# Sums of the value weights on POOL, other places for splits, statistics and x sums, and the feature minimum taken from the differences

## The chip, the core and the metric

The kernel runs on one core of a Trainium2 chip. The core has five engines with queues of their own: TensorE (PE; its weight loads are shown as PEld), VectorE (DVE), ScalarE (ACT), GpSimd (POOL) and SyncE (SP), which here only issues transfers; ACT issues a few too. Each engine works off its instructions in order and waits on semaphores for the others. The metric is device time in microseconds (us) of the whole kernel.

## The reference: what is computed

For 2048 tokens of width 640, the reference normalizes x and lets two branches work on it. The first is linear attention with 32 heads of 20: queries and keys go through a small matrix per head and a double softmax, and the sums over all tokens of (key feature times value) and of the key features give the output. The second is a two-layer GELU network of width 1536. The result is x + s * silu(g).

```
xn = _layernorm(x, axis=-1)
phi_q = concatenate([_softmax(pq), _softmax(-pq)]);  phi_k likewise     # per head, over 20
kv = einsum("bhsf,bhsd->bhfd", phi_k, v);  z = einsum("bhsf->bhf", phi_k)
o  = (phi_q kv) / (phi_q z + 1e-6);        s = o @ wo
g  = silu(gelu(xn @ w1 + b1) @ w2 + b2)
return x + s * g
```

## The kernel before

Everything is float32 in value, but TensorE works on pairs of fp32r halves: a tile is copied rounded by ACT (high half), and DVE or POOL subtract to get the rest (low half); `PASSES` multiplies high by high, high by low and low by high. "Split" below means this pair of instructions.

The tokens are worked off in 16 tiles of 128; a pair q is tiles 2q and 2q+1. Tiles 0 to 9 are projected one by one (`project`, 30 matmuls of 320 columns). For tiles 6 to 9 each turn t does a key tile, a value tile and two query tiles. From tile 10 on (passes p = 5, 6, 7, the loop over `range(5, 8)`), keys are still done tile by tile, but the values of a pair are done together in `token_pair` by a scheme of seven products (parts X, Y, X, V, Z, W, Z) on sums and differences of weights and of x. The same scheme then does the queries of pairs 4 to 7, and the feed-forward part over 12 units fills the rest of the time.

For the scheme, four sums of the value weights are made by `v_forms(0)` and `v_forms(1)` (each loads two 128-row blocks, makes four sums of 320 columns and stores the blocks to `sv_dram`). `forms` reloads them as four tiles and splits them, one per `next`: the first two are the tiles `ws` of parts Y and V, the last two go partly into the old `wv` tiles (part W) and partly into a third `ws` (the second part Z). The query weights take the same way through `sq_dram`; `w_dump` stores two `wq` tiles for a later reload. For x, `pair_stats` makes a tile's mean and variance (DVE) and reciprocal deviation (POOL, a power), sends both through `st_dram` and reads them back on all partitions as `bc`; `pair_sub` (POOL) and `pair_mul` (DVE) normalize the pair `xr`; `pair_plain` splits it into `xp`; `t_sums` (five POOL instructions) makes its x sums and `t_split` splits them into `xd`.

`feat1` makes the exponents of a tile from the PSUM tile `pA`: per head maximum `mx` and minimum `mn`, differences to the maximum, `nr` = minimum less maximum, and on POOL the second half (`nr` less differences); `feat2` is ACT's exponential, `key_fin` the division by the sums (the product on POOL). There are three PSUM tiles `pA` in turn (`bankA`); TensorE can start a fourth projection only when the features, or ACT's eviction of a value tile, have read the oldest.

Order: TensorE's and SP's instructions in this phase go out as the program writes them (`manual_schedule` on these two engines). On DVE, ACT and POOL, Tile's scheduler sets the order from the program and its own estimate; from the feed-forward part on, all is as written. In `value_pair(p, {...})` the dictionary hooks pieces of other work behind numbered parts of the scheme.

## Time and profile before

Times are device microseconds.

| | |
|---|---|
| median of 3 runs | 663.66 (662.34 to 664.63) |
| profiled execution | 663.49, of which 661.4 is the span from the first to the last instruction |
| mean granted TensorE clock | 0.994 of full |
| busy in the span: PE, PEld | 648.8 (98%), 562.4 |
| DVE, ACT, POOL | 501.6 (76%), 237.4 (36%), 395.5 (60%) |
| moved by DMA | 135.15 MB, 204 GB/s mean |

How to read what follows: a row of the timeline gives start, duration, engine, line of the program, operation, output and inputs, shapes and how many instructions are merged; in brackets, how long the engine had been idle before and whose work ended that. The duration of merged rows is from the first start to the last end; a single instruction's duration overlaps the next one's by some 0.08 us. "SPq" and "ACTq" rows are transfers being issued. In the chain of waits, each piece is what released the next. A line "a/b/c" gives the shortest, median and longest duration in ns.

### The profile page before, as it was taken

The numbers are of one execution on the slowest core, as the hardware profiler recorded it, in microseconds if no ns is written. First come the engines' busy times: TensorE is split into PE (matmuls) and PEld (weight loads), VectorE is DVE, ScalarE is ACT, GpSimd is POOL, SyncE is SP. The second block draws the span as 40 slices with busy tenths as digits, with TensorE's granted clock in tenths as the row PEclk, the third lists the DMA queues.
The fourth block names the chain that finished last, engine by engine and source line by source line (L and its number), as shares of the span: only waits on it lengthen the run. The fifth ranks groups of instructions, "written<-read, shape, count | busy, mean of one in ns | idle before, by whom it ended". The sixth has DMA issues, their size and how long they took to land.

```text
span 661.4 us, 11452 instructions
## 1 busy us (share of the span) xinstructions
PE 648.8 (98%) x4396; PEld 562.4 (85%) x4396; DVE 501.6 (76%) x777; ACT 237.4 (36%) x345; POOL 395.5 (60%) x351
## 2 busy tenths in 40 slices
PE   9999999989799999999999999999999999999997
PEld 9999999989799998888888888888888887766866
DVE  5785977998887988758978868859789899853232
ACT  3512322413534256352442444841322425132130
POOL 2755475787586855857778776363462967343321
PEclk9999999999799999999999999999999999999999
DMA  9706297533811168628799699796779399999952
GB/s 349 273 1 175 83 345 227 128 123 124 198 58 42 70 227 290 210 76 282 194 278 324 154 402 323 128 327 241 147 214 244 85 266 183 310 232 254 299 208 79
DMA packets 164447, 135.15 MB, mean 204 GB/s; under 512 B 89394, under 2 KB 128562, under 8 KB 164010
## 3 DMA queue, kind: packets, MB, share of 16 engines
q1 hardware_dynamic: 161658, 122.84, 63.6%
q10 hardware_dynamic: 2736, 11.60, 5.3%
q8 instruction: 34, 0.56, 0.4%
q14 instruction: 19, 0.16, 0.1%
HBM read 86.03 MB, written 48.38 MB: 203 GB/s over the span
## 4 chain that ended last, share of the span: by engine, by line
PE 81%; DVE 5%; DMA 5%; POOL 4%; issue 2%; SPq 1%; ACT 1%; ACTq 0%; DVEq 0%; POOLq 0%
PE pB L909 24%; PE pB L880 22%; PE pA L371 11%; PE pB L1067 11%; PE pA L653 5%; DMA st_dram<-pst 2%; PE pB L1014 2%; PE pA L174 1%; POOL xr L301 1%; PE qV L653 1%; PE kv L453 1%; DMA folds<-in_wqk_dram 1%; POOL e L414 1%; POOL e L392 1%; PE qY L653 1%
## 5 line engine op out<-in xcount | busy, mean ns | idle before, releaser
L909 PE MATMUL pB<-hs,w2s 128*128 128x512 f32 x720 | 165.8, 389 | 0.0
L909 PEld LDWEIGHTS pB<-hs,w2s 128*128 128x128 f32 x720 | 135.0, 188 | 28.8 <-DVE y L918 0.8
L880 PE MATMUL pB<-xp,w1s 128*128 128x512 f32 x324 | 81.4, 390 | 0.0
L880 PE MATMUL pB<-xd,w1s 128*128 128x512 f32 x324 | 79.3, 389 | 0.0
L1067 PE MATMUL pB<-oT,wo 128*128 128x512 f32 (+1 forms) x315 | 72.3, 381 | 0.0
L880 PEld LDWEIGHTS pB<-xp,w1s 128*128 128x128 f32 x324 | 60.7, 188 | 12.8 <-DVE pB L1148 0.3
L880 PEld LDWEIGHTS pB<-xd,w1s 128*128 128x128 f32 x324 | 60.8, 188 | 12.6
L414 POOL TENSOR_TENSOR eq<-eq,rc 128x1280 f32<-128x1280 f32 x16 | 37.9, 2370 | 55.9 <-DVE rc L971 38.7
L1067 PEld LDWEIGHTS pB<-oT,wo 128*128 128x128 f32 x315 | 57.2, 188 | 13.8 <-PE pB L1014 2.5
L918 DVE TENSOR_TENSOR y<-pB,y 128x512 f32<-128x512 f32 x100 | 63.1, 675 | 1.4 <-PE pB L909 1.4
L401 ACT ACTIVATE e<-e 128x1280 f32<-128x1280 f32 x32 | 40.6, 1270 | 65.5 <-POOL e L392 65.5
L392 POOL TENSOR_TENSOR e<-nr,e 128x640 f32<-128x640 f32 x32 | 46.4, 1449 | 23.5 <-DVE nr L391 18.0
L414 POOL TENSOR_TENSOR e<-e,rc 128x1280 f32<-128x1280 f32 x16 | 39.2, 2450 | 35.0 <-DVE rc L441 35.0
L371 PE MATMUL pA<-wk,xp 128*128 128x320 f32 x384 | 59.7, 310 | 0.3 <-ACT v L430 0.3
L885 ACT ACTIVATE pB<-pB,b1t 128x512 f32<-128x512 f32 x48 | 31.8, 662 | 78.7 <-DVE pB L1148 28.9
L371 PEld LDWEIGHTS pA<-wk,xp 128*128 128x128 f32 x384 | 56.9, 188 | 0.7 <-ACT v L430 0.6
L958 POOL TENSOR_TENSOR ez<-eq,zrep 128x1280 f32<-128x1280 f32 x16 | 47.3, 2959 | 1.4 <-DMA eq<-e_dram 1.4
L481 POOL TENSOR_TENSOR w1s<-raw,w1s 128x640 fp32r<-128x640 f32 (+1 forms) x18 | 26.8, 1489 | 31.9 <-ACT w1s L480 31.9
L371 PE MATMUL pA<-wv,xp 128*128 128x320 f32 x240 | 37.7, 311 | 0.0
L371 PEld LDWEIGHTS pA<-wv,xp 128*128 128x128 f32 x240 | 35.5, 188 | 0.1
L1070 POOL TENSOR_TENSOR xres<-gt,xres 128x256 f32<-128x256 f32 x20 | 14.3, 737 | 35.3 <-DVE gt L1069 24.8
L891 DVE TENSOR_TENSOR hs<-pB,hs 128x512 fp32r<-128x512 f32 x48 | 32.0, 683 | 3.9 <-ACT hs L887 3.7
(182 smaller groups left out, 1159.8 us busy)
## 6 DMA issues: line engine op xcount, KB each, us to landing
raw<-in_w_dram SPq DMA_DIRECT2D x42, 320.0 KB
e_dram<-e ACTq DMA_DIRECT2D x16, 640.0 KB
eq<-e_dram SPq DMA_DIRECT2D x16, 640.0 KB
phi_t<-eq SPq DMA_DIRECT2D x64, 160.0 KB
phT<-phi_t SPq DMA_DIRECT2D x20, 480.0 KB
xt<-in_x_dram SPq DMA_DIRECT2D x16, 320.0 KB
xres<-in_xt_dram SPq DMA_DIRECT2D x20, 256.0 KB
out_dram<-xres SPq DMA_DIRECT2D x18, 256.0 KB
```

Source lines behind the costliest of these rows:

```text
L371: nc.tensor.matmul(ps[:, hf, :HALF], stat_x(q, o, k, a), ws[k][:, b, hf * HALF:(hf + 1) * HALF], start=n == 0, stop=n == 3 * KC - 1)
L392: rest = lambda: nc.gpsimd.tensor_tensor(e5[:, :, :, 1, :], nr[:, :, :, None].to_broadcast([P, 2, 16, DH]), e5[:, :, :, 0, :], op=OP.subtract)
L401: nc.scalar.activation(ef, ef, AF.Exp)
L414: nc.gpsimd.tensor_tensor(e3, e3, rc[:, :, None].to_broadcast([P, 64, DH]), op=OP.mult)
L653: nc.tensor.matmul(bank[ch], q_x(blk, a, q), p_weight(base, f, w, k)[:, b], start=ch not in seen and n == 0, stop=n == len(mms) - 1, skip_ ...
L880: nc.tensor.matmul(bank[ch][:], tl[:, a, off + wo_:off + wo_ + P], mov(blk, b), start=new and n == 0, stop=n == len(mms) - 1, skip_group_c ...
L885: nc.scalar.activation(ps, ps, AF.Gelu_apprx_tanh, bias=b1t[:, f:f + 1])
L891: nc.vector.tensor_tensor(hs[:, 1], ps, hs[:, 0].bitcast(F32), op=OP.subtract)
L909: nc.tensor.matmul(ps[:], ws[i][:, b, d * P:(d + 1) * P], hs[o][i][:, a, :], start=i == n == 0, stop=(i, n) == (GF - 1, 2), skip_group_che ...
L918: nc.vector.tensor_tensor(y, ps[:], y, op=OP.add)
L958: nc.gpsimd.tensor_tensor(zv, ef, zf, op=OP.mult)
L1067: nc.tensor.matmul(ps[:, mv], w, o[:, mv], start=n == 0, stop=n == 15, skip_group_check=True)
```

## The change

1. `v_forms`: both groups of four sums run on POOL (before, the second ran on DVE). The second group's loads and sums go to turn 6 (before: turns 7 and 8).
2. `feat1`: the minimum over `pA` and the subtraction of two 128x32 tiles go; instead `nr` is the minimum over the differences `e`, read from SBUF. The result is the same, since subtracting the maximum keeps the order.
3. `XIN`, `STATS`: tiles 14 and 15 are loaded at the end of turn 7 (before 8), their statistics made in turn 8 (before 9).
4. Turns 7 to 9: `t_sums` comes behind the first query's features. In turn 9, the first two splits of the reloaded sums are made there (before in pass p=5), ahead of `t_split`; in pass p=5 one fewer in the hook and one fewer behind the key.
5. `w_dump`: both stores of `wq` go to turn 9, behind the reload of the sums (before: turns 6 and 7).
6. Pass p=7: the last of the four query splits is POOL's and comes at part 2 (before DVE, part 5).

```diff
 def v_forms(i):
-        eng = nc.vector if i else nc.gpsimd
-        put = lambda d, x, y, op: eng.tensor_tensor(d, x, y, op=op)
+        put = lambda d, x, y, op: nc.gpsimd.tensor_tensor(d, x, y, op=op)
...
 def feat1(ps, later=None):
-        mn = small.tile([P, 2, 16], F32, tag="mn", name="mn")
         nc.vector.tensor_reduce(mx[:], p4, axis=AX.X, op=OP.max)
-        nc.vector.tensor_reduce(mn[:], p4, axis=AX.X, op=OP.min)
...
-        last_feat[0] = nc.vector.tensor_tensor(nr[:], mn[:], mx[:], op=OP.subtract)
+        last_feat[0] = nc.vector.tensor_reduce(nr[:], e5[:, :, :, 0, :], axis=AX.X, op=OP.min)
...
-    XIN = {6: (12, 13), 8: (14, 15)}
-    STATS = {6: (10, 11), 7: (12, 13), 9: (14, 15)}
+    XIN = {6: (12, 13), 7: (14, 15)}
+    STATS = {6: (10, 11), 7: (12, 13), 8: (14, 15)}
...
         if t == 9:
             vb = forms(sv_dram, wv_f, wv_s, [nc.vector] * 4)
             next(vb)
+            w_dump(0)
+            w_dump(1)
         if t == 6:
+            next(vf[1])
             spill(3)
...
+        pq = project(next(queries), wq_s)
+        ef = feat1(pq)
         if t > 6:
             t_sums(q - 1)
-        pq = project(next(queries), wq_s)
-        ef = feat1(pq)
         if t < 9:
             pair_mul(q)
-        if t in (7, 8):
-            next(vf[1])
...
         ef = feat1(pq)
+        if t == 6:
+            next(vf[1])
+        if t == 9:
+            next(vb)
+            next(vb)
         if t > 6:
             t_split(q - 1)
...
-        if t in (6, 7):
-            w_dump(t - 6)
...
-            qf = forms(sq_dram, wq_f, wq_b, [nc.vector] * 4)
+            qf = forms(sq_dram, wq_f, wq_b, [nc.vector, nc.vector, nc.vector, nc.gpsimd])
...
         if p == 5:
             load_xr(7)
             next(vb)
-            next(vb)
...
         def rest(t=t, p=p):
-            if p == 5:
-                next(vb)
...
-        value_pair(p, {0: lambda: p == 5 and next(vb), 1: rest, 5: lambda: p == 7 and next(qf), 4: first_key, 6: second_key})
+        value_pair(p, {0: lambda: p == 5 and next(vb), 1: rest, 2: lambda: p == 7 and next(qf), 4: first_key, 6: second_key})
```

TensorE's instructions keep their order. On the others, three places matter. In the rows below, `mx`, `mn`, `e` and `nr` belong to one feature computation, `xr<-xr,bc` is the multiplication of a pair, `raw<-raw` the sums of the value weights, `st` and `pst` the statistics.

DVE in turn 8, before: between the first and the second query's features.

```order
L345 TENSOR_TENSOR xr<-xr,bc 128x1280
L214 TENSOR_TENSOR raw<-raw 128x320 x4
L384 TENSOR_REDUCE mx<-pA 128x32
L385 TENSOR_REDUCE mn<-pA 128x32
L388 TENSOR_TENSOR e<-pA,mx 128x32x20
L391 TENSOR_TENSOR nr<-mn,mx 128x32
```

The same place after the change (the last four rows stand there once more, for the second tile, and then come the second query's features):

```order
L344 TENSOR_TENSOR xr<-xr,bc 128x1280
L230 BN_STATS st<-xt 128x6 x2
L231 BN_AGGR st<-st 128x2
L232 TENSOR_SCALAR pst<-st 128x1
L235 COPY pst<-st 128x1
```

The sums have left DVE, the statistics of tiles 14 and 15 (from turn 9) stand there.

ACT from the first query of turn 9 into pass p=5, before (`e` is an exponential, `xd` the x split, `ws` and `wv` the copies of the reloaded sums, `qx` the copy of a PSUM part):

```order
L401 ACTIVATE e<-e 128x1280
L685 DMA e_dram<-e 128x1280
L322 ACTIVATE xd<-xr 128x9x128
L401 ACTIVATE e<-e 128x1280
L685 DMA e_dram<-e 128x1280
L609 ACTIVATE ws<-raw 128x640 x2
L657 ACTIVATE qx<-pA 128x320
L609 ACTIVATE wv<-raw 128x320
L609 ACTIVATE ws<-raw 128x320
```

The same place after:

```order
L398 ACTIVATE e<-e 128x1280
L682 DMA e_dram<-e 128x1280
L606 ACTIVATE ws<-raw 128x640 x2
L321 ACTIVATE xd<-xr 128x9x128
L398 ACTIVATE e<-e 128x1280
L682 DMA e_dram<-e 128x1280
L606 ACTIVATE wv<-raw 128x320
L606 ACTIVATE ws<-raw 128x320
L654 ACTIVATE qx<-pA 128x320
```

The copies of the first two sums have moved ahead of the x split and of the second exponential, and those of the third ahead of the copy of the first PSUM part.

POOL in turn 8, before (`xr<-xr` are the x sums, `e<-nr,e` the second half of the exponents, `e<-e,rc` the key product):

```order
L414 TENSOR_TENSOR e<-e,rc 128x1280
L301 TENSOR_TENSOR xr<-xr 128x2x128 x4
L301 TENSOR_TENSOR xr<-xr 128x128
L392 TENSOR_TENSOR e<-nr,e 128x32x20 x2
L323 TENSOR_TENSOR xd<-xr,xd 128x9x128
L392 TENSOR_TENSOR e<-nr,e 128x32x20
```

The same place after:

```order
L411 TENSOR_TENSOR e<-e,rc 128x1280
L389 TENSOR_TENSOR e<-nr,e 128x32x20
L300 TENSOR_TENSOR xr<-xr 128x2x128 x4
L300 TENSOR_TENSOR xr<-xr 128x128
L233 TENSOR_TENSOR pst<-pst,mhalf 128x1 x2
L389 TENSOR_TENSOR e<-nr,e 128x32x20
L322 TENSOR_TENSOR xd<-xr,xd 128x9x128
L389 TENSOR_TENSOR e<-nr,e 128x32x20
```

The first query's exponents come ahead of the x sums, and the two powers of the statistics come between the sums and the second query's exponents.

## The prediction

> **What bounds the kernel now.** I read the page first, then busy time by stretches, then what TensorE waited for, then the rows around those waits.
>
> ```profile
> span 661.4 us, 11452 instructions
> PE 648.8 (98%) x4396; PEld 562.4 (85%) x4396; DVE 501.6 (76%) x777; ACT 237.4 (36%) x345; POOL 395.5 (60%) x351
> ```
>
> TensorE is busy for 648.8 of 661.4 us, so only its 12.6 us of idle time and any slowed clock can be won. The next view cuts the span into stretches; the columns are the length, then the busy time of PE, weight loads, DVE, ACT and POOL, and the granted clock.
>
> ```profile
> core 0: us, PE busy (x) PEld busy (x) DVE busy (x) ACT busy (x) POOL busy (x), PEclk, DMA share, GB/s
> 165.00:176.40 11.40, 7.68 (x32) 6.67 (x33) 8.50 (x12) 8.38 (x13) 7.64 (x9) 0.70 0.96 212
> 300.00:661.40 361.40, 357.07 (x1588) 283.54 (x1586) 263.67 (x402) 124.07 (x186) 204.54 (x156) 1.00 0.83 235
> ```
>
> The last 361 us lose 4.3 us, at the end, and the change does not reach there. The sore place is 165 to 176.4: TensorE sits idle for 3.7 us and then runs at clock 0.70. Next, all waits of TensorE's matmuls in its middle part (total, times, longest):
>
> ```profile
> PE qY L653 <- ACT ws L609: 2.6, 1, 2.6
> PE pA L371 <- DVE nr L391: 2.0, 1, 2.0
> PE qY L653 <- DVE ws L610: 1.1, 2, 0.6
> PE pA L653 <- DVE pA L667: 1.0, 1, 1.0
> PE pA L371 <- ACT v L430: 0.3, 1, 0.3
> ```
>
> So three places count: 143 us (a bank that the features free late), 165 us (split weights `ws`), 223 us (a sum in the first query pair). TensorE's order of instructions is the same in both kernels; what the change can do is take away such waits or make new ones.
>
> **Place B, the splits of the sums of the value weights.** TensorE, the chain of waits, ACT and DVE:
>
> ```profile
> 154.57 4.67 PE L371 MATMUL pA<-wk,xp 128*128 128x320 f32 x30 [0.34 <-ACT v L430]
> 179.91 8.80 PE pA L371 x60
> 198.15 8.80 PE pA L371 x60
> 163.40 1.28 ACT L401 ACTIVATE e<-e 128x1280 f32<-128x1280 f32 x1 [8.88 <-POOL e L392]
> 167.88 1.36 ACT L609 ACTIVATE ws<-raw 128x640 fp32r<-128x640 f32 x2 [0.48 <-ACT e L401]
> 168.65 2.85 DVE L610 TENSOR_TENSOR ws<-raw,ws 128x640 fp32r<-128x640 f32 x2 [2.90 <-ACT ws L609]
> ```
>
> Pass p=5 (two key tiles, one sum into kv, one value pair) runs on TensorE from 154.57 to 179.91, 25.34 us; pass p=6, the same matmuls, from 179.91 to 198.15, 18.24 us. The 7.1 us between them are what late `ws` costs, slow clock included. ACT stood idle 8.88 us for POOL and only then worked off exponentials, x splits and `ws` in order. After the change statistics 14 and 15 are gone from DVE there, POOL makes the second operand of the first query's exponential ahead of the x sums instead of behind them, ACT copies `ws` ahead of the x split and of the second query's exponential, and DVE splits `ws` ahead of key tile 10's features. If `ws` is then in time: -7.1.
>
> **Place A, sums of the value weights off DVE.**
>
> ```profile
> 137.35 5.51 DVE L214 TENSOR_TENSOR raw<-raw 128x320 f32<-128x320 f32 x4
> 158.52 0.87 DVE L231 BATCH_NORM_STATS2 st<-xt 128x6 f32<-128x320 f32 x2
> 161.08 0.81 DVE L384 TENSOR_REDUCE mx<-pA 128x32 f32<-128x640 f32 x1
> 145.20 4.63 PE L371 MATMUL pA<-wq,xp 128*128 128x320 f32 x30 [2.00 <-DVE nr L391]
> ```
>
> The four sums fill 137.35 to 142.86; only then come the features whose bank TensorE needs at 143.2. In their place now stand statistics 14 and 15, 2.56 us (158.52 to 161.08), so those features start near 139.9 and release the bank (behind maximum and difference) about 1.6 us later, 141.5. The 2.0 us wait goes: -2.0.
>
> On POOL the four sums go in at tile 6, behind the second query's exponent operand. POOL's time for the first pair's sums is in the trace, and its cover is its idle time before the x subtraction of the next pair:
>
> ```profile
> L214 POOL TENSOR_TENSOR raw<-raw x4: 878/882/888, 77.5 to 80.4; 128x320 f32<-128x320 f32 x4
> 110.25 2.99 POOL L340 TENSOR_TENSOR xr<-xr,bc 128x1280 f32<-128x1280 f32 x1 [3.86 <-issue]
> ```
>
> Four of them cost between 3.5 us (0.88 each) and 5.5 us (the DVE row above, taken in turns with POOL); I take 3.5, POOL's own row. They fill that gap, cost 0. Without the gap they would move the x subtraction and all behind it on POOL by as much. The loads are issued on SP ahead of two stores of `xp`; the two stores of `wq` leave the place between the broadcasts `bc` and go behind the reload of the sums. Nobody reads them before p=7, so both cost 0.
>
> What speaks against it is that DVE instructions with two SBUF inputs can stand still while POOL works (rows below), so that sums on POOL may cost DVE what they save it. By the rows the gain stays: what is freed is DVE's queue ahead of a bank that TensorE needs, while POOL's turn for the sums lies some 30 us earlier, where TensorE waits for nothing. The Trainium skill, "Perfetto Trace Analysis", section "Optimizing Scalar/DVE Operations", says that moving work between DVE and GPSIMD might not help because they share an SBUF port; by that rule A would give 0 and the sum below would be 2.0 us worse.
>
> **The minimum from the differences.** A reduction from PSUM and a tiny subtraction, 32 times each, become one reduction of the differences in SBUF, which stands third instead of second.
>
> ```profile
> L391 DVE TENSOR_TENSOR nr<-mn,mx x32: 174/180/2670, 21.3 to 255.1; 128x32 f32<-128x32 f32 x32
> L409 DVE TENSOR_REDUCE rc<-e x16: 1472/1480/1487, 29.2 to 220.9; 128x64 f32<-128x1280 f32 x16
> 124.64 2.70 POOL L323 TENSOR_TENSOR xd<-xr,xd 128x1152 fp32r<-128x1152 f32 x1 [0.62 <-ACT xd L322]
> 124.71 2.67 DVE L391 TENSOR_TENSOR nr<-mn,mx 128x32 f32<-128x32 f32 x1
> ```
>
> The subtraction takes 0.18 us but up to 2.67, exactly as long as the POOL instruction that had started before it. A reduction that reads one SBUF tile (L409, 1280 numbers) takes 1.472 to 1.487 us in all 16 cases, under POOL or not. So the new reduction of 640 numbers lies between 0.74 us (half of L409) and 1.48 (strided reads at half speed); I take 0.81, what the maximum of the same count takes from PSUM (row 161.08), nearest in size. Feature time without POOL stays about 2.3 us, and the stretched cases shrink by up to 2.5 us. The bank is free one instruction (0.73 us) earlier. None of this is on TensorE's path by itself, so it counts 0 in the sum, and it is the margin for what follows.
>
> **Place C, the last quarter of the query splits on POOL.**
>
> ```profile
> 216.85 2.60 DVE L610 TENSOR_TENSOR wqb<-raw,wqb 128x320 fp32r<-128x320 f32 x1
> 219.37 1.17 DVE L610 TENSOR_TENSOR ws<-raw,ws 128x320 fp32r<-128x320 f32 x1
> 223.92 1.14 PE L653 MATMUL pA<-ws,xp 128*128 128x320 f32 x6 [0.96 <-DVE pA L667]
> 216.74 2.37 POOL L414 TENSOR_TENSOR e<-e,rc 128x1280 f32<-128x1280 f32 x1 [3.87 <-DVE rc L441]
> ```
>
> DVE loses 3.6 us of work right ahead of the sum that TensorE waits 0.96 us for; POOL takes two instructions in a gap of 3.87 us. -1.0. Without the gap the key product behind them is late, which TensorE reads only two query pairs on.
>
> **What is late next.** POOL is now the tight queue of tiles 8 and 9. Its rows, and ACT's eviction of the last value tile:
>
> ```profile
> 132.92 2.99 POOL L340 TENSOR_TENSOR xr<-xr,bc 128x1280 f32<-128x1280 f32 x1 [3.67 <-DMA wq_dram<-wq]
> 135.99 3.67 POOL L414 TENSOR_TENSOR e<-e,rc 128x1280 f32<-128x1280 f32 x1
> 148.11 2.69 POOL L323 TENSOR_TENSOR xd<-xr,xd 128x1152 fp32r<-128x1152 f32 x1 [1.60 <-ACT xd L322]
> 158.50 3.63 POOL L301 TENSOR_TENSOR xr<-xr 128x256 f32<-128x256 f32 x5
> 162.09 1.28 POOL L392 TENSOR_TENSOR e<-nr,e 128x640 f32<-128x640 f32 x1
> 163.32 1.06 POOL L234 TENSOR_TENSOR pst<-pst,mhalf 128x1 f32<-128x1 f32 x2
> 153.83 0.68 ACT L430 ACTIVATE v<-pA 128x640 f32<-128x640 f32 x1
> ```
>
> Laid end to end in the new order from 135.9: key product 3.67, operand 1.28, x sums 3.63, powers 1.06, operand 1.28, x split 2.69, operand of key 9 1.28: 150.8. ACT's exponential (1.28) and the eviction follow: 152.8. TensorE wants that bank for key tile 10 at 154.57 - 0.34 - 2.0 = 152.2. A wait of 0.6 stands where 0.34 stood: +0.3. From 152.1 DVE makes key 9's sums (1.48 and a reciprocal, to 154.1), POOL the product, the operand, the x sums and the next operand (about 8.6 us, to 162.7), ACT an exponential, two half copies and the copy of bank X, to 165.4. TensorE, at key 10 from 152.8, wants bank X again at 152.8 + 8.8 (both key tiles) + 1.5 (the kv sums, what pass p=6 has left beside 60 and 54 matmuls at 8.80 / 60 each) + 1.8 (parts X and Y) = 164.9: +0.5. `ws` itself is there earlier: ACT copies it behind the first query's exponential near 160.5, DVE is through by 163, and part Y starts near 163.9. These 0.8 us vanish if `bc` lands sooner without the store of `wq` behind it, which is the wait that row 132.92 names, and double if POOL meets DVE more often.
>
> The reloaded sums must also be there. They now stand behind the last statistics on SP:
>
> ```profile
> 88.91 5.09 DMA xt<-in_x_dram
> 164.41 0.37 SPq L332 DMA_DIRECT2D st_dram<-pst  x1
> 169.61 0.32 SPq L334 DMA_DIRECT2D bc<-st_dram  x1
> ```
>
> Powers end near 145.5, the store's round trip to `bc` takes 5.2 us, four issues about 2, a load 5.1: 157.8, against ACT's turn near 159.
>
> **The sum.** -2.0 (A) - 7.1 (B) - 1.0 (C) + 0.3 + 0.5 = -9.3. The profiled execution took 663.49 us (2.1 around its span; 0.17 under the median 663.66): 654.2.
>
> **Rivals.** *The stall moves to POOL's chain.* For it: POOL is in order and each operand now waits for more. Against: every wait above is under 1 us. If half of place B comes back, 3.5 us: 657.7. From 2 to 6 us lost: 656 to 660.5. *The reduction is dear* (1.48 us). Then each feature costs 0.7 more on DVE, ten of them between 133 and 165 cost 7, and 661 to 662 results; L409's even rows speak against it. *POOL holds DVE up:* the sums at tile 6 cost DVE's x splits 3.5 us in waits as in row 124.71, and the bank at 143 is as late as before: 656.2. *Slower:* the reloads of the sums land late, behind `bc` on SP's in-order queue. Part Y wants `ws` near 163.9, and copy and split need some 4 us after the landing; each us past 160 is lost on TensorE, and a wait of 3.7 us drew 7.1 - 3.7 = 3.4 us of slow clock with it in the row of 165 to 176.4. A landing at 166 (6 us of wait and 3.4 of slow clock) eats the whole gain; at 169 the time is 666.5. The loads would have to take 13 us in place of 5.1.
>
> **How the numbers follow.** Forecast 0.72 (652.6 to 656), moved stall 0.14, dear reduction 0.04 (no change), POOL holding DVE up 0.04 (655 to 657), slower 0.06. The low end is all waits gone and no new one (653.4) less the spread of runs; the high end, 658.5, takes in half of B. Faster by over 0.3% (2 us, about what runs of this kernel tell apart): 0.90; within it 0.04; slower 0.06.
>
> **What would show it.** Right: TensorE's waits on `ws` gone, passes p=5 and p=6 equally long, clock 1.00 throughout, the new reduction at about 0.8 us in all 32 cases with no long ones, the wait at 143 gone. Wrong: TensorE waiting on ACT's copy of bank X or on `ws` behind a DMA, POOL without idle time from 133 to 165, or a reduction well over 0.8.

## The result

The changed kernel takes 660.65 us (median of 13 runs, 659.70 to 662.23), the kernel before 664.45 (13 runs beside them): ratio 0.9954, 95% interval 0.9941 to 0.9967: a gain of 3.8 us by the medians and of 3.1 us by the ratio. Forecast were 654.2 us and a range up to 658.5. The direction was right, the size was not, and the time lies outside the range.

The profiled execution of the changed kernel took 661.99 us. From its page, the span and the busy times; then TensorE's waits in its middle part (total, times, longest):

```profile
span 660.3 us, 11417 instructions
PE 649.2 (98%) x4396; PEld 562.6 (85%) x4396; DVE 493.0 (75%) x739; ACT 237.6 (36%) x345; POOL 399.2 (60%) x357
```

```profile
PE pA L370 <- DVE e L385: 2.3, 2, 1.9
PE pA L650 <- ACT qx L654: 1.5, 2, 1.0
PE pA L650 <- DVE wv L607: 1.0, 1, 1.0
PE pA L650 <- DVE v L664: 0.9, 2, 0.6
```

The waits for `ws` and the wait at 223 us are gone, as forecast. The wait near 143 us is still there (1.86 us at 146.17), pass p=5 has new ones for `qx`, `wv` and `v`, and pass p=6 has two. TensorE's timeline shows where:

```profile
146.17 6.17 PE L370 MATMUL pA<-wq,xp 128*128 128x320 f32 x30 [1.86 <-DVE e L385]
156.57 4.56 PE L370 MATMUL pA<-wk,xp 128*128 128x320 f32 x30
169.34 1.58 PE L650 MATMUL pA<-wv,xp 128*128 128x320 f32 x9 [0.52 <-ACT qx L654]
173.84 1.89 PE L650 MATMUL pA<-wv,xd 128*128 128x320 f32 x11 [1.02 <-DVE wv L607]
176.31 1.15 PE L650 MATMUL pA<-ws,xp 128*128 128x320 f32 x6 [0.58 <-DVE v L664]
177.74 4.56 PE L370 MATMUL pA<-wk,xp 128*128 128x320 f32 x30
190.94 1.58 PE L650 MATMUL pA<-wv,xp 128*128 128x320 f32 x9 [0.95 <-ACT qx L654]
```

Pass p=5 runs from 156.57 to 177.74, 21.17 us (before: 25.18 by the same rows). Pass p=6 runs from 177.74 to 197.75, 20.01 us (before: 18.24, without a wait). The span is only 1.1 us shorter than before; two more profiles of the changed kernel, taken with the experiments, have spans of 660.8 and 658.6. The next table puts three of the four side by side. Its first row is the start of POOL's product for key tile 9, for a reason that the experiments give; the spans between are worked out from the starts of the rows named.

| us | before | changed, first profile | changed, third profile |
|---|---|---|---|
| POOL's product of key 9 starts | 156.18 | 156.84 | 155.16 |
| from there to the end of pass p=5 | 23.57 | 20.90 | 20.89 |
| pass p=6 | 18.24 | 20.01 | 20.01 |
| pass p=7 and the queries, to the feed-forward part | 52.62 | 51.43 | 51.42 |
| feed-forward part and end | 410.79 | 411.12 | 411.12 |
| span | 661.4 | 660.3 | 658.6 |

The change won 2.7 us behind POOL's product (place B) and 1.2 us in the queries (place C), lost 1.8 in pass p=6, and moved the product itself by +0.7 or -1.0 (place A was to bring it 2 us forward). The profiled execution of before (663.49 us) and the third of the changed kernel (660.32) lie 3.2 us apart, the first one (661.99) only 1.5; the medians, 3.8. The profiled execution of before is 0.96 us under its kernel's median of 13, and the first of the changed kernel 1.34 us above its own, which makes up the difference. Not all of the gain lies in the instructions, either: outside the span, the kernel before spends 2.1 us on average and the changed kernel 1.7. No run shows why.

### The profile page after: what moved, and what is told of

The parts are those of the page before. It is cut to its first block, busy times and chain, and to the rows that moved or that the text cites. A ratio compares the mean times of both kernels' runs of the same rounds, so it can differ in the third digit from the quotient of the medians.

```text
span 660.3 us, 11417 instructions
## 1 busy us (share of the span) xinstructions
PE 649.2 (98%) x4396; PEld 562.6 (85%) x4396; DVE 493.0 (75%) x739; ACT 237.6 (36%) x345; POOL 399.2 (60%) x357
## 4 chain that ended last, share of the span: by engine, by line
PE 84%; DVE 6%; POOL 5%; ACT 1%; issue 1%; DMA 1%; SPq 0%; ACTq 0%; DVEq 0%; POOLq 0%
PE pB L907 24%; PE pB L878 21%; PE pA L370 14%; PE pB L1065 11%; PE pA L650 5%; PE pA L174 2%; PE pB L1012 2%; POOL e L389 2%; POOL e L411 1%; POOL xr L300 1%; DVE xp L287 1%; PE qV L650 1%; PE kv L450 1%; ACT e L398 1%; DVE rc L406 1%
## 5 line engine op out<-in xcount | busy, mean ns | idle before, releaser
L478 POOL TENSOR_TENSOR w1s<-raw,w1s 128x640 fp32r<-128x640 f32 (+1 forms) x18 | 25.0, 1391 | 29.4 <-ACT w1s L477 23.3
```

## The experiments

Each kernel was run in five rounds beside the kernel before on the same chip, except the third profile of the changed kernel, which is a single execution. "Ratio" is to the kernel before; "product" is the start of POOL's product of key 9, "behind it" the time from there to the end of pass p=5. Each ratio comes from 6 to 12 executions of the kernel, while span, product and passes are those of one profile. Every kernel in the table, whatever its edit, spends 1.7 to 1.8 us outside its span and the kernel before 2.1, so that 0.3 to 0.4 us (about 0.0005 of the ratio) speak for each of them without any change between the first instruction and the last. Where it matters, the mean span of all executions is given beside the ratio.

| kernel | ratio (95%) | span | product | behind it | p=6 |
|---|---|---|---|---|---|
| changed, again | 0.9956 (0.9939 to 0.9973) | 660.8 | 157.37 | 20.88 | 20.01 |
| x sums of turn 7 early | 0.9976 (0.9965 to 0.9987) | 659.3 | 155.87 | 20.95 | 19.96 |
| x sums of turns 7 to 9 early | 1.0013 (1.0002 to 1.0024) | 661.6 | 156.22 | 22.84 | 19.96 |
| sums on POOL alone | 1.0008 (0.9995 to 1.0021) | 662.8 | 157.74 | 23.01 | 18.24 |
| split on DVE | 0.9988 (0.9975 to 1.0000) | 663.3 | 159.77 | 20.98 | 20.01 |
| x sums of turn 9 late | 0.9947 (0.9932 to 0.9962) | 659.4 | 156.74 | 20.05 | 19.95 |
| all three | 0.9927 (0.9912 to 0.9942) | 656.4 | 156.24 | 19.56 | 18.35 |
| eviction first | 0.9929 (0.9907 to 0.9950) | 656.5 | 156.21 | 19.54 | 18.40 |
| `wv` splits first | 0.9918 (0.9900 to 0.9936) | 656.2 | 155.82 | 19.16 | 18.80 |
| query split alone | 0.9981 (0.9968 to 0.9994) | 661.1 | 156.40 | 24.17 | 18.23 |
| old minimum | 0.9950 (0.9934 to 0.9966) | 658.0 | 156.31 | 20.99 | 18.35 |
| minimum alone | 1.0020 (1.0009 to 1.0030) | 662.2 | 155.14 | 23.34 | 19.71 |
| operand held | 0.9988 (0.9976 to 1.0000) | 661.0 | 157.54 | 20.92 | 19.97 |
| operand held, second form | 0.9924 (0.9907 to 0.9940) | 658.2 | 156.29 | 20.92 | 18.44 |

### The wait near 143 us: a buffer, and then POOL

DVE's timeline of the changed kernel, turn 8. The second query of turn 7 has its maximum at 118.88, but its differences start only here:

```profile
124.79 0.82 DVE L385 TENSOR_TENSOR e<-pA,mx 128x640 f32<-128x640 f32 x1 [5.09 <-DMA e_dram<-e]
132.55 3.46 DVE L287 TENSOR_TENSOR xp<-xr,xp 128x384 fp32r<-128x384 f32 x1
144.35 0.81 DVE L382 TENSOR_REDUCE mx<-pA 128x32 f32<-128x640 f32 x1
```

They waited 5.09 us for a store: their tile `e` (from the pool of 23 large buffers) got the buffer of the first query's `e`, which is free only when that one is stored. In the kernel before the differences of that query start at 121.69 without such a wait. Which buffer a tile gets is decided by Tile when it sets the order, and moving `t_sums` behind the first query's features is enough to change it, as the next run shows. First theory: this wait is why the gain of place A is missing. The test moves the x sums of turn 7 back:

```
-        pq = project(next(queries), wq_s)
-        ef = feat1(pq)
-        if t > 6:
+        if t == 7:
+            t_sums(q - 1)
+        pq = project(next(queries), wq_s)
+        ef = feat1(pq)
+        if t > 7:
             t_sums(q - 1)
```

> The changed kernel, with the x sums of turn 7 alone back ahead of the first query's features; turns 8 and 9 as changed. Theory S (buffer): in the changed kernel the differences `e` of turn 7's second query get the buffer of the first query's `e` and wait 5.09 us on DVE for that tile's store; the wait at 139.2 (0.48 us), the one at 144.3 (1.86 us) and the 1.5 us of slow clock behind it are its price. In this order the differences take another buffer: the 5.09 us are gone although the first query's store is issued later, TensorE's waits between 139 and 147 fall under 0.5 us in all, and pass p=5 starts near 153 instead of 156.6: 656.7 (4 us less than 660.65). Rival L (lock): DVE is late there because POOL's instructions with two SBUF inputs hold its splits (3.46 us for one of 0.55); then the wait at 144 stays above 1 us and the time within 1 us of 660.65.

The mechanism came out as expected, the time did not. TensorE and ACT of that kernel:

```profile
154.26 4.66 PE L370 MATMUL pA<-wk,xp 128*128 128x320 f32 x30 [2.07 <-ACT v L427]
168.37 1.58 PE L650 MATMUL pA<-wv,xp 128*128 128x320 f32 x9 [1.76 <-ACT qx L654]
```

```profile
152.35 1.27 ACT L398 ACTIVATE e<-e 128x1280 f32<-128x1280 f32 x1 [1.30 <-POOL e L389]
153.52 0.69 ACT L427 ACTIVATE v<-pA 128x640 f32<-128x640 f32 x1
```

Between 100 and 154 us TensorE now has no wait at all. It waits 2.07 us at 154 instead, for ACT's eviction of v9, which stands behind an exponential that waited for POOL; and `qx` costs 1.76 in place of 0.52. The ratio, 0.9976, is no better than the changed kernel's. Rival L fares no better: DVE's last split took 0.55 us here. With the x sums early in turns 8 and 9 too (`if t > 6` in place of `if t == 7` above, and the second call gone) the result is worse still:

> The changed kernel with the x sums of turns 7, 8 and 9 back ahead of the first query's features. Theory S: the 5.09 us wait on DVE is gone as in the run with turn 7 alone (-4), but in turn 9 POOL makes the operand of the first query's exponential some 3.6 us later, ACT's copies of `ws` come that much later, and part Y waits up to 3 us for them: 657 to 660. If the order in turn 9 is of no use to place B, 656.7 as with turn 7 alone. Rival L: 660 to 664.

It took 663.42 us, 1.0013 of the kernel before. The late x sums of turns 8 and 9 are therefore worth 1.9 us behind POOL's product (22.84 against 20.95, slow clock included), and behind that product only those of turn 9 stand: that part of the forecast for place B holds.

Second theory, P: not TensorE but POOL's in-order queue, with ACT and DVE in between, sets the pace from 112 to 175 us; TensorE has slack there, and a wait of it is worth nothing. One test is place A alone: the kernel before, with only the second group of sums on POOL in turn 6.

```
 def v_forms(i):
-        eng = nc.vector if i else nc.gpsimd
-        put = lambda d, x, y, op: eng.tensor_tensor(d, x, y, op=op)
+        put = lambda d, x, y, op: nc.gpsimd.tensor_tensor(d, x, y, op=op)
...
         if t == 6:
+            next(vf[1])
             spill(3)
...
-        if t in (7, 8):
-            next(vf[1])
...
         ef = feat1(pq)
+        if t == 6:
+            next(vf[1])
```

> The kernel before, with only the second group of sums of the value weights on POOL in turn 6 (place A alone; the queries' and statistics' order, the minimum and all splits as before). Prediction's count for A: the wait of 2.00 us at 145.2 goes and nothing comes back, -2.0. Theory P (POOL's chain is the bound right behind it): the wait at 145 goes, but TensorE, earlier by as much, waits longer for v9's eviction (0.34 before) and for `ws` (3.7 before): less than 1 us is won. Rival from the Trainium skill, Perfetto Trace Analysis, section Optimizing Scalar/DVE Operations (a move between DVE and GPSIMD might not help): by that rule 0 too, but then with the wait at 145 still in place.

The wait of 2.00 us at 145 is gone, and a larger one stands at the next place (TensorE's timeline):

```profile
156.13 6.91 PE L370 MATMUL pA<-wk,xp 128*128 128x320 f32 x30 [4.43 <-ACT v L429]
```

Ratio 1.0008 (mean span 0.7 us longer than before): place A alone won nothing. The forecast's cited rule (the Trainium skill, "Perfetto Trace Analysis", section "Optimizing Scalar/DVE Operations") gave 0 too, and the measurement agrees with that result; but the wait at 145 did go.

Two things took the gain back, and this run does not separate them. One is theory P: the eviction that TensorE waits for stands behind POOL's operand. The other is a cost that the forecast set to 0, the loads of the second group, which SP now issues earlier. Pair 5's statistics are ready at 98.74 us before and at 98.45 here, but SP is still at work on what stands ahead of their store (SP's queue, before and place A alone):

```profile
98.77 0.37 SPq L332 DMA_DIRECT2D st_dram<-pst  x1
```

```profile
100.44 0.91 SPq L331 DMA_DIRECT2D st_dram<-pst  x1
```

POOL's x subtraction, which needs them back, starts at 112.75 in place of 110.25, and the product of key 8 at 138.19 in place of 135.99; the chain of waits of this kernel runs over these transfers. All 14 profiles with the moved loads, those of the changed kernel included, issue this store 0.2 to 2.4 us after the statistics are ready, the three without them (before, query split alone, minimum alone) 0.02 to 0.03 us after. What place A would be worth without this delay, no run shows. DVE's splits beside the moved sums had a smaller price: in turn 7 of the changed kernel they took 0.95, 1.10 and 1.63 us (0.82, 0.42 and 0.56 before).

The chain of waits shows theory P without an experiment. Of the changed kernel, in order of time:

```profile
138.14 2.30 POOL e L411
...
151.43 1.86 POOL e L389
153.31 1.28 ACT e L398
154.62 1.50 DVE rc L406
...
156.84 2.37 POOL e L411
...
173.31 0.49 DVE wv L607
173.84 1.91 PE pA L650 x11
```

From 112.9 to 173.8 it holds no piece of TensorE. The same view of the kernel before was there to be read:

```profile
136.04 3.62 POOL e L414
...
150.80 1.82 POOL e L392
152.65 1.28 ACT e L401
153.96 1.50 DVE rc L409
...
168.52 0.72 ACT ws L609
...
171.55 0.90 PE qY L653 x2
```

It holds none of TensorE between 98.8 and 171.5; the wait at 145 is not on it.

### The same kernel three times

> The changed kernel once more, beside the next three kernels on one chip: 3 to 4 us under the kernel before, as measured. All other numbers of this set are told against this run.

> A third profile of the changed kernel. Theory P: however TensorE loses time at 139 to 152 (two profiles lost 2.3 us in waits there, the one with and the other without 1.54 us of slow clock), pass p=5 ends 177.7 to 178.3 in all of them, because its waits take up the difference; span 660 to 661. If TensorE's own losses count, the end of p=5 moves by as much as they differ.

The third profile refutes one half of its expectation and supports the other. Pass p=5 ended at 176.05, not between 177.7 and 178.3, and the span is 658.6, not 660 to 661. But in all three profiles it ends 20.88 to 20.90 us behind the start of POOL's product of key 9 (table), although TensorE's own losses ahead of p=5 differ: waits of 0.48 and 1.86 us and 1.5 us of slow clock in the first, 0.64, 0.38 and 1.85 us at full clock in the second, 1.03 us in the third. The waits for `qx` take up the difference (0.52, 1.74 and 1.76). Five more kernels of the table have the same order of work behind that product (x sums of turn 7 early, split on DVE, old minimum, and the two with the operand held): there it starts at 155.87 to 159.77, and p=5 ends 20.92 to 20.99 us behind it.

What made the third one quicker is who began first at 132 us. POOL subtracts the mean of pair 6 as soon as `bc` has landed. The first profile (POOL's timeline), then the third (POOL's, and DVE's):

```profile
132.31 3.28 POOL L339 TENSOR_TENSOR xr<-xr,bc 128x1280 f32<-128x1280 f32 x1
```

```profile
133.37 3.00 POOL L339 TENSOR_TENSOR xr<-xr,bc 128x1280 f32<-128x1280 f32 x1 [1.20 <-DMA bc<-st_dram]
```

```profile
132.38 0.55 DVE L287 TENSOR_TENSOR xp<-xr,xp 128x384 fp32r<-128x384 f32 x1
```

In the first, POOL starts 0.24 us ahead of DVE's last split, which then takes 3.46 us (row 132.55 above) until POOL is through; DVE's key sums and POOL's product of key 8 come as much later. In the third, POOL waits 1.20 us for `bc` and starts 1.1 us later, DVE's split is through in 0.55, and the product of key 9 starts 1.7 us earlier. A transfer that came later made the kernel quicker. The second profile has the order of the first (POOL at 132.94, DVE's split at 133.18 with 3.36 us) and a product of key 9 as late (157.37). This is read from three traces; no run changed this order alone.

### Making POOL's chain shorter

Three edits on top of the early x sums of turn 7. First, the low half of turn 8's x split on DVE, which stood idle there:

```
-            t_split(q - 1)
+            t_split(q - 1, nc.vector if t == 8 else nc.gpsimd)
```

> As the kernel with the early x sums in turn 7, and the low half of turn 8's x split (2.70 us on POOL at 147.8) made by DVE, which stands idle for 4.32 us there. Theory P (POOL's chain is the next bound): the operand of key 9, ACT's exponential and the eviction of v9 come some 2 us earlier, and TensorE's wait of 2.07 us for that eviction falls under 0.5; the whole chain of turn 9 behind it moves along, so that the wait for `qx` stays about 1.8: some 2 us under the kernel with the early sums alone, 1.5 to 2.5 under the changed kernel in the profile's span. Rival D (DVE or the transfers set the pace): the wait for the eviction stays above 1.5 us.

Theory P was right in one half: the wait for the eviction went. But the time did not fall, because DVE's split stands ahead of the second query's features in DVE's order and waits for ACT's copy, which waits for POOL's x sums (DVE, then TensorE):

```profile
149.66 2.25 DVE L322 TENSOR_TENSOR xd<-xr,xd 128x1152 fp32r<-128x1152 f32 x1 [3.23 <-ACT xd L321]
```

```profile
153.64 3.40 PE L370 MATMUL pA<-wq,b 128*128 128x320 f32 x12 [3.29 <-DVE e L385]
```

DVE's idle time was not free time: what stands behind the moved instruction waits with it. Ratio 0.9988, a loss of some 2 us against the changed kernel beside it (0.9956). Second, in turn 9 the x sums behind both queries' operands and their split in pass p=5:

```
-        if t > 7:
+        if t == 8:
             t_sums(q - 1)
...
-        if t > 6:
+        if t in (7, 8):
             t_split(q - 1)
         store_e(queries_done.pop(0), ef)
+        if t == 9:
+            t_sums(q - 1)
...
             feat2(es[t])
+            if p == 5:
+                t_split(6)
```

> As the kernel with the early x sums in turn 7; in turn 9 the x sums come behind both queries' exponent operands, and their split goes into pass p=5 behind the sixth-pair's first exponential (nobody reads it before pass p=6). Theory P: ACT's second exponential of turn 9 no longer waits for POOL's x sums (4.20 us), so that the waits for `qx` (1.76 us) and for the split of `wv` (1.08 us) in p=5 go; the wait of 2.07 us for the eviction of v9 stays: 2 to 2.8 us under the kernel with the early sums alone. Rival A (ACT's own queue: four copies of `wv` and `ws` ahead of `qx`): the wait for `qx` stays above 1 us.

The wait for `qx` in p=5 is gone, as theory P expects; that for `wv` is smaller but not gone (0.65 us in place of 1.08), and the wait for the eviction stays, 2.39 us with a clock of 0.76 from 154 to 161 us. Against the early x sums alone the ratio falls from 0.9976 to 0.9947, some 2 us. The two profiles do not show it: the spans are 659.3 and 659.4, because POOL's product came 0.9 us later in the second one, while p=5 ends 0.9 us sooner behind it. All three edits, with the old minimum:

> Early x sums in turn 7, DVE's split in turn 8, late x sums in turn 9, and the old feature code. Theory P with a price for the new minimum (in p=6 POOL's operand gets ahead of DVE's multiplication: 2.56 us in place of 1.49, and 0.95 and 0.29 us of waits): all waits of TensorE between 139 and 200 under 1 us in all, span 655 to 656.5, 4 to 5 us under the changed kernel. If the new minimum is free, the old one in its place wins nothing over the parts: 656.5 to 658. If POOL's chain is not the bound, 659 or more.

The profile's span of 656.4 us lies within the expectation, the rest does not. TensorE waits 3.31 us at 150.87 (DVE's split again) and 0.42 us for `v`, in place of under 1 us in all; and over six executions the mean span is 657.7 us, 2.2 us under that of the changed kernel beside it, where 4 to 5 were expected. Ratio 0.9927. The DVE split was then replaced by a move of one instruction: in turn 9 ACT evicts v9 ahead of key 9's exponential, in a kernel with the late x sums and the old minimum.

```
+        if t == 9:
+            vs[t] = value(t)
         feat2(es[t])
-        vs[t] = value(t)
+        if t < 9:
+            vs[t] = value(t)
```

> As the kernel with early x sums in turn 7 and late x sums in turn 9, with the old feature code, and in turn 9 ACT's eviction of v9 ahead of key 9's exponential in place of behind it. Theory P: ACT no longer holds v9's bank until POOL's operand and the exponential are through; the wait at 154 (2.39 us, with 1.55 us of slow clock behind it in the run without this) goes, some 1 to 2 us of it come back as a wait for `qx` or `wv` in p=5, because POOL's chain itself is not shorter, and p=6 runs in 18.35 us: span 654.5 to 656.5, 5 to 7 us under the kernel before. If the eviction waits for something else (the bank's own projection, a buffer), the wait stays and the span is 657 to 658.5.

As theory P expects: ACT evicts at once, TensorE starts p=5 at 152.65 without a wait, and most of it comes back inside p=5, as a wait of 1.12 us for DVE's features ahead of key 11's projection and as a longer one for `wv` (ACT, then TensorE):

```profile
151.28 0.69 ACT L429 ACTIVATE v<-pA 128x640 f32<-128x640 f32 x1
152.68 1.27 ACT L400 ACTIVATE e<-e 128x1280 f32<-128x1280 f32 x1 [0.71 <-POOL e L391]
```

```profile
171.86 1.88 PE L652 MATMUL pA<-wv,xd 128*128 128x320 f32 x11 [2.39 <-DVE wv L609]
```

POOL's product starts at 156.21 as ever, and p=5 ends 19.54 us behind it, as in the kernel with all three. The last edit, on top of the eviction first, makes DVE's fourth split of the sums ahead of key 11's features:

```
             load_xr(7)
             next(vb)
+            next(vb)
...
-        value_pair(p, {0: lambda: p == 5 and next(vb), 1: rest, ...})
+        value_pair(p, {1: rest, ...})
```

> As the kernel with the eviction first, and in pass p=5 the fourth split of the sums (second half of `wv` and third `ws`) made on DVE ahead of key tile 11's features in place of behind them. Theory Q (DVE's in-order queue holds the split: 171.32 there, features from 169.03): the wait of 2.39 us for `wv` at 171.9 and the 0.60 behind it go, p=5 becomes 2 to 3 us shorter; key 11's features come 2 us later on DVE but TensorE is earlier too, so that p=6 may wait up to 1 us for `qx`: span 654 to 655.5, 7 to 9 us under the kernel before. Rival P2 (POOL's chain sets the end of p=5, at 175.8 in two kernels with other waits): the wait moves to `v` or `qx` and the span stays at 656 to 657.

The rival came closer: the wait for `wv` is gone, waits of 0.37 (`qx`), 0.68 and 0.87 us (`v`) stand in its place, and the span is 656.2. The end of p=5 did move, from 19.54 to 19.16 us behind the product, but p=6 took 0.4 us more. Ratio 0.9918, the lowest here, 5 us under the kernel before; the next three, at 0.9924 to 0.9929, do not differ from it by more than they are uncertain. One of its six executions took 1666.71 us, which the ratio leaves out and no profile explains.

### The minimum from the differences

The forecast counted it 0. Twice it was tested: the changed kernel with the old `feat1`, and the kernel before with the new one (the part of the change's diff that touches `feat1`, undone and alone).

> The changed kernel with the old feature code (minimum from PSUM, small subtraction). Theory S: the buffer that the second query of turn 7 gets is the same as in the changed kernel, so the wait of some 5 us on DVE stays, and the time stays within 1.5 us of 660.65. Rival M (the new reduction's dependence): three dependent steps of 0.85 us in place of 0.73 us steps cost DVE 0.1 to 0.15 us per feature and are what makes the banks late: 657 to 659.

> The kernel before with the new feature code alone. Prediction's count: 0, the time stays at 664.45 within 1. Rival M: 0.1 to 0.15 us more per feature, ten features ahead of `ws`: 665 to 666. Third way: the bank is free one instruction earlier and stretched subtractions (up to 2.67 us) are gone, 662 to 663.

The old code in the changed kernel keeps the waits at 139 and 146 (0.33 and 1.97 us), so the buffer does not hang on it; p=6 falls from 20.01 to 18.35 us, while the two ratios (0.9950, 0.9954) do not differ by more than they are uncertain. The new code in the kernel before costs 1.3 us by its ratio and 2.1 us by the mean spans: the bank at 144 does come free earlier (a wait of 0.79 us in place of 2.00, POOL's product at 155.14), and p=6, 19.71 us, more than takes it back. By the time, rival M (665 to 666) was right; but its cause, banks that are late, is not what the trace shows. The main cause lies at one place of p=6. The changed kernel (DVE, then POOL), and the one with the old minimum (DVE, then POOL):

```profile
184.06 0.82 DVE L388 TENSOR_REDUCE nr<-e 128x32 f32<-128x640 f32 x1
186.51 2.56 DVE L344 TENSOR_TENSOR xr<-xr,bc 128x1280 f32<-128x1280 f32 x1 [1.63 <-POOL xr L339]
```

```profile
186.42 1.29 POOL L389 TENSOR_TENSOR e<-nr,e 128x640 f32<-128x640 f32 x1
```

```profile
184.10 1.94 DVE L390 TENSOR_TENSOR nr<-mn,mx 128x32 f32<-128x32 f32 x1
186.03 1.49 DVE L344 TENSOR_TENSOR xr<-xr,bc 128x1280 f32<-128x1280 f32 x1
```

```profile
186.19 2.47 POOL L391 TENSOR_TENSOR e<-nr,e 128x640 f32<-128x640 f32 x1 [0.19 <-DVE nr L390]
```

With the old code the small subtraction cannot run beside POOL's x subtraction and ends with it. POOL's next instruction, the operand, needs its result, so DVE's multiplication of the last pair begins first and takes 1.49 us. The new reduction is through long before; POOL's operand begins 0.09 us ahead of the multiplication, which then takes 2.56. ACT's copies of that pair, and behind them `qx`, come later by as much: the wait of 0.95 us at 190.94. The stretched subtraction, whose disappearance the forecast took for margin, was a brake that held POOL back at the right moment. Theory W says just that; the test puts POOL's operand by hand behind the sum of parts X and Y.

```
-        es[t] = feat1(pk)
+        es[t] = feat1(pk, held if p == 6 else None)
...
+            if p == 6:
+                held.pop(0)()
             later.pop(0)()
             feat2(es[t])
```

> The changed kernel, with POOL's operand for key tile 12 (pass p=6) put behind the sum of the first two parts, so that POOL does nothing beside DVE's multiplication of the last pair. Theory W (who gets to work first): the multiplication takes 1.49 us instead of 2.56, TensorE's wait of 0.95 us for `qx` in p=6 and the 0.29 us for `v` go, p=6 takes 18.3 to 18.6 us in place of 20.0, and the time falls by 1 to 1.6 us against the changed kernel. Rival M2 (the three dependent steps of the new feature code are what makes p=6 late): the multiplication is shorter, but a wait of 0.5 us or more stays in p=6 and the time falls by less than 0.7 us.

The multiplication took 1.49 us and the wait for `qx` went, but TensorE waited 1.36 us for the eviction of the first value bank, which in ACT's order stands behind the held exponential. By its numbers (ratio 0.9988) the rival M2 would have it. Part of that ratio is not p=6's: the store that the differences of turn 7 wait for ended later (they start at 126.05 in place of 124.79), and the product with it, at 157.54. So the exponential was moved behind that eviction as well, from part 1's hook into part 2's:

```
             later.pop(0)()
-            feat2(es[t])
+            if p != 6:
+                feat2(es[t])
...
+        def third(t=t, p=p):
+            if p == 6:
+                feat2(es[t])
+            if p == 7:
+                next(qf)
...
-        value_pair(p, {..., 2: lambda: p == 7 and next(qf), ...})
+        value_pair(p, {..., 2: third, ...})
```

> As the kernel with the held operand, and ACT's exponential of key 12 behind the eviction of the first value bank in place of ahead of it (there the eviction waited 1.36 us behind that exponential). Theory W: the multiplication takes 1.49 us, no wait for `qx`, `v` or the eviction over 0.3 us stays in p=6, which takes 18.3 to 18.7 us in place of 20.0; the time falls by 1 to 1.6 us against the changed kernel (to 4.5 to 5.5 us under the kernel before). Rival M2 (the dependent reductions themselves are late): a wait of 0.5 us or more stays in p=6, on a result of DVE.

DVE of that kernel:

```profile
183.53 0.82 DVE L388 TENSOR_REDUCE nr<-e 128x32 f32<-128x640 f32 x1
185.93 1.49 DVE L344 TENSOR_TENSOR xr<-xr,bc 128x1280 f32<-128x1280 f32 x1 [1.58 <-POOL xr L339]
```

No wait is left in p=6, which takes 18.44 us, and the ratio is 0.9924: theory W holds, and in p=6 the new reduction itself is not what costs. A smaller cost stays: from the feed-forward part to the end, the ten profiles with the new reduction take 411.10 to 411.23 us and the seven with the old code 410.70 to 410.86. The cause of these 0.3 us was not tested.

### The last quarter of the query splits

> The kernel before, with only the last of the four query splits on POOL at part 2 (place C alone). Prediction's count: the wait of 0.96 us at 223.9 goes, -1.0. Rival: POOL holds the split and the key product behind it up, and the wait moves: 0.

```
-            qf = forms(sq_dram, wq_f, wq_b, [nc.vector] * 4)
+            qf = forms(sq_dram, wq_f, wq_b, [nc.vector, nc.vector, nc.vector, nc.gpsimd])
...
-        value_pair(p, {..., 5: lambda: p == 7 and next(qf), ...})
+        value_pair(p, {..., 2: lambda: p == 7 and next(qf), ...})
```

TensorE has no wait there any more; the first query pair takes 7.92 us (217.02 to 224.94) in place of 9.14, and from pass p=7 to the feed-forward part 1.1 us are won (51.55 for 52.62). The ratio, 0.9981, is 1.3 us, of which 0.4 lie outside the span; the mean span is 0.7 us shorter. Place C came out as forecast, as nearly as these runs can tell.

## Why the prediction was right or wrong

- **Right.** Place C: -1.0 forecast, -1.2 in the changed kernel's trace; alone -1.1 in the trace and -1.3 by the ratio. The waits on `ws` are gone, and the reloaded sums were in time. The reduction takes 0.82 us in all 32 cases (row below), forecast 0.81. The sums on POOL took 4.22 us, between the bounds given, and POOL's idle time behind them is still 3.82.

```profile
L388 DVE TENSOR_REDUCE nr<-e x32: 819/820/822, 21.0 to 253.3; 128x32 f32<-128x640 f32 x32
```

- **Wrong: place A, "The 2.0 us wait goes: -2.0".** Two things failed in this step. The features started at 144.35, not 139.9, because DVE was held by the buffer (5.09 us) and by POOL's subtraction (3.46). And without them (early x sums, and the sums on POOL alone, there with the delay of the next point) the wait went and nothing was won: it was a wait of the busiest engine, but not on the chain. The forecast read TensorE's list of waits and took each for time that can be won; the chain of waits of the same profile runs over POOL from 110 to 171 us. On that chain something was won and lost again: from the product of key 8 to that of key 9 the changed kernel takes 18.70 to 18.72 us in its three profiles, before 20.19, but the product of key 8 starts 0.5 to 2.7 us later.
- **Wrong: the moved loads, "so both cost 0".** They held the store of the statistics back by 0.7 to 2.0 us in the three profiles of the changed kernel (0.02 before), and POOL's x subtraction of pair 5 starts at 111.87 to 112.29 in place of 110.25. That is part of why the product of key 8 is late.
- **Wrong: place B, "If `ws` is then in time: -7.1".** It was in time, and the stretch became 2.7 us shorter, not 7.1. The comparison with pass p=6 supposed that nothing else would be late at 18.24 us. `qx`, `wv` and `v` were (0.52 to 1.76, 1.0 and 0.6 us): TensorE waiting for ACT's copy of bank X was one of the forecast's own signs of being wrong. The clock was 1.00 in p=5, as claimed, but not throughout (0.72 behind the wait at 146.17 in the first profile). The 7.1 itself mixes rows of two views; on TensorE's timeline, where p=6 starts at 179.75, the difference of the passes before is 6.9.
- **Mis-sized: what is late next, +0.3 and +0.5.** This was the right chain. It was laid out to end with key 9's operand at 150.8; measured are 153.3, 153.8 and 151.6 in three profiles and 152.3 with the early x sums. The product of key 8 began at 138.14 (136.44 in the third) in place of 135.99, because the x subtraction and DVE's sums ahead of it were late, and an operand beside DVE took 2.46 and 1.91 us in place of 1.28. With TensorE really early the eviction's wait was 2.07 us, not 0.6. The two terms stood at 0.8; the chain took back all of place A and 2.9 us of place B (21.17 against 18.24).
- **Wrong: the minimum, "it counts 0 in the sum".** +1.8 us in p=6, where POOL's operand now begins ahead of DVE's multiplication, and +0.3 in the feed-forward part; alone +1.3 by the ratio. What was taken for margin, the end of the stretched subtractions, is what cost p=6 its good order.
- **The rivals.** "The stall moves to POOL's chain" (0.14; 656 to 660.5) named the mechanism, and the measured 660.65 is just past its end. "POOL holds DVE up" happened in a small part: DVE's splits beside the moved sums took 1.9 us more in all, not 3.5. "The reduction is dear" is not what happened, and the reloads were not late.

By the forecast's terms: A 0 in place of -2.0, B -2.7 in place of -7.1 with the two terms behind it, C -1.2, the minimum +1.8 and +0.3 (with it a wait of 0.23 us in the feed-forward part that the kernel before does not have): -1.8 in all. The place of POOL's product adds -1.0 in the third profile (span -2.8) and +0.7 in the first (-1.1).

## What to carry to other kernels

Look at the chain of waits in the stretch in question before counting a wait of the busiest engine as time to be won: if the chain runs over other engines there, the wait will be waited at the next place, and the measure of success is when the chain's own instruction starts (here POOL's product: behind it the end of the pass stood fixed to 0.02 us in three profiles). Moved transfers belong to such a chain as well: a load issued earlier on an in-order queue holds back the small store behind it (here by up to 2.4 us). A tile that comes from a rotating pool carries a hidden edge: where a change moves instructions, the waits of each row that allocates a tile are to be compared, not only the rows' places. And an instruction that is slowed by its neighbour may be what keeps two others in the good order: before it is made faster, look at who starts next.

## What the runs showed of the hardware

- Two instructions with two SBUF operands, one on DVE and one on POOL, did not share: the one that began first, by as little as 0.09 or 0.24 us, ran in nearly its own time (1.29 us for 1.28, 3.28 for 2.99), and the other took longer by most of that (1.49 became 2.56, 0.55 became 3.46). The Trainium skill, "SBUF — State Buffer", section "SBUF: two separate sides", says that whichever starts first gets the shared pair for the whole instruction and the other blocks; the rows agree. What was not expected is that, as far as three traces show, this decides between 658.6 and 660.3 us of span for one and the same kernel.
- A DVE instruction that needs the result of the one ahead of it starts 0.85 to 0.86 us behind that one's start, one that does not 0.73 to 0.74 (changed kernel 159.00, 159.85, 160.71; before 161.08, 161.82, 162.55): the new order of the three steps costs some 0.25 us per feature beside the operation itself.
- A wait of 1.86 us on TensorE was followed by 30 matmuls in 6.17 us at a granted clock of 0.72 in the first profile of the changed kernel, a wait of 1.85 us at the same place by 4.63 us at 1.00 in the second. No run shows what decides between the two.
